# Infini-attention and MLP in one kernel: causal mask as half-array products, MLP output halves in tiles of their own, spare PSUM banks at the end, small work from VectorE to ScalarE, and a new order

## The chip, the cores and the metric

One core of a Trainium2 chip. The metric is the device time of one execution in microseconds (us), as the median of three runs. Lower is better.

## The reference

Inputs: q, k, v of shape (4, 8, 576, 64), a memory matrix `M_prev` and a norm `z_prev` for each head, a gate `beta`, and two matrices of an MLP, 512 x 2048 and 2048 x 512. Both stages work on all 4 x 576 = 2304 tokens.

```python
scores = scale * np.matmul(q, k.transpose(0, 1, 3, 2))
scores = np.where(causal, -1000000000.0, scores)
scores = scores - scores.max(-1, keepdims=True)
a = np.exp(scores); a /= a.sum(-1, keepdims=True) + 1e-09
local = np.matmul(a, v)
q_p = phi(q)                       # phi(x) = where(x > 0, x, exp(x) - 1) + 1
mem_out = einsum(q_p, M_prev) / (einsum(q_p, z_prev)[..., None] + 1e-06)
x = g * mem_out + (1 - g) * local  # g = sigmoid(beta), one per head; then heads side by side: (2304, 512)
h = x @ w_in
gelu = where(h >= 1, h, where(h <= -1, 0, (h + 1) ** 2 / 4))
out = gelu @ w_out
```

## The kernel before

**Numbers.** Every f32 operand of a product is split into two f16 tiles, a high and a low half ("hi" and "lo"), and a product is three f16 passes (`PASSES`). Splitting costs two passes over the data: `mul` writes hi (ScalarE, line 109, or VectorE, line 112) and `sub_scaled` writes lo (VectorE, line 116). Powers of two that keep f16 in range come from sums of squares (line 204, 328, 602).

**Work.** Weights come in 8 groups `W0` to `W7` (`weight_group`: three integer passes on VectorE at lines 201 to 203, then hi and lo). Heads come in 8 pairs of units (`P0` to `P7`, `prep`: hi and lo of q, k, v, M, and phi with its norm, lines 349 to 385) and 16 units of two heads. A unit has a half A (query tiles 0 and 1) and a half B (tiles 2, 3 and 4). For one query tile, `front` makes the scores on TensorE (line 413, or 439 and 441 for the short last tile; the two heads' products use 64 rows of the array each and run side by side), adds the causal mask with a product of `ident` and `mask` (line 458; all 128 rows), takes the row maximum on VectorE (line 462, 444), scales it (`negmax`, line 424, VectorE), and takes the exponential and its sum on ScalarE (line 428). `back` multiplies by the inverse sum and splits into hi and lo, and a DMA transposes them. `pv1` and `pv2` multiply with v (line 533; two 64-column halves side by side).

The MLP runs in 9 chunks `c0` to `c8` of 256 tokens, each over 8 groups of 256 hidden columns: 24 products into `h` (`mlp_h`, line 646, one PSUM bank, and there is one such bank), the activation in five passes (line 651 Relu and 652 Square on ScalarE, line 653 the clamp with max and min on VectorE, then hi on ScalarE and lo on VectorE; "16th Relu" below counts them in order of time), and 12 products into `o` (`mlp_o`, line 663, one tile of two banks). A chunk ends with two reads of `o` (line 690 or 692) and two output DMAs.

**Order.** The string `PROGRAM` lists the jobs, which only gives a first order. `in_order` then prices every instruction, plays the program forward and back under a list of blends, and fixes the order of each engine's own queue by the best round. Every engine runs its queue strictly in that order.

**Lines that the change touches.** Line 350 (`prep`) is the minimum of exp and 1 on VectorE; `negmax` is line 424; the mask products are lines 437 and 458; `halves` chooses the engine of hi by `OPT["hi"]`, which sends column groups 6 and 7 (the two heads of tile 3, 128 x 512) to VectorE; `mlp_h` and `chunk` hold the tiles `h` and `o`.

```python
OPT = dict(whi="act", phi="act", ghi="act", hi={6: "dve", 7: "dve"})
```

Of the kernel before, what the change touches and what calls it, by code (L numbers as in the profile page):

```python
# [49 lines left out]
def infini_moe_kernel(ctx: ExitStack, tc, qt, kt, qz, vm, beta, w, out):  # L50
# [92 lines left out]
    def setup_consts():  # L143
# [7 lines left out]
        nc.gpsimd.memset(mask, 0.0)  # L151
        nc.gpsimd.affine_select(out=mask, in_=mask, pattern=[[-1, P]], base=0,
                                channel_multiplier=1, compare_op=ALU.is_ge, fill=MASK)

        nc.gpsimd.tensor_copy(mask4[0:D], mask[0:D, 0:D])
        nc.gpsimd.tensor_copy(mask4[D:P], mask[D:P, D:P])
# [477 lines left out]
    def mlp_h(c, r, a, tb):  # L634
# [16 lines left out]
        nc.scalar.activation(tm, h, AF.Relu, bias=tb[:, 1, j:j + 1], scale=tb[:, 2, j:j + 1])  # L651
# [254 lines left out]
def in_order(tc, notes):  # L906
# [61 lines left out]
    for blend in BLENDS:  # L968
        times, taken = forward(urgency)
        end = max(t[1] for t in times)  # L970
        if end < best:
            best, order = end, taken
# [55 lines left out]
```

## Time and profile before

| | us |
|---|---|
| median of 3 runs (lowest to highest) | 617.37 (616.97 to 619.64) |
| the profiled execution's own time | 617.87 |
| its span, first to last instruction | 616.2 |
| busy: TensorE, VectorE, ScalarE | 521.7, 475.5, 451.8 |
| mean granted TensorE clock | 0.952 of full |

PE is TensorE's products, PEld its weight loads, DVE VectorE, ACT ScalarE, POOL GpSimd. A busy time is the time in which at least one instruction of the engine runs, so it is less than count times mean where instructions overlap. The profiled execution lies 0.50 us above the median, and its own time 1.67 us above its span.

### The profile page before, as it was taken

How to read it: one execution, taken by the hardware profiler on the slowest of the kernel's cores; microseconds unless marked ns; L12 is line 12 of the kernel's file. 1: busy time of each engine (PE TensorE's matmuls, PEld its weight loads, DVE VectorE, ACT ScalarE, POOL GpSimd, SP SyncE). 2: the span in 40 equal slices, each digit the busy share in tenths (PEclk: the TensorE clock that was granted, in tenths of full speed). 3: DMA queues.
4: the chain of work that ended last, by engine and by line, in shares of the span. 5: the costliest groups of instructions: out<-in, count | busy, mean ns of one | idle time of the engine just before them, and what ended most of it. 6: DMA issues, size and time to landing. Idle time of an engine off the chain costs nothing. (4 is left out here: it accounts for less than half of the span.)

```text
span 616.2 us, 11580 instructions
## 1 busy us (share of the span) xinstructions
PE 521.7 (85%) x4481; PEld 333.6 (54%) x4481; DVE 475.5 (77%) x1106; ACT 451.8 (73%) x916; POOL 2.5 (0%) x12
## 2 busy tenths in 40 slices
PE   0324565768699999999999999999999999999996
PEld 0112334444456566656665665666666666666663
DVE  5999999999999998497989849978677763223221
ACT  5768877769989987599797879769886765444433
POOL 1000000000000000000000000000000000000000
PEclk9997655799899999999999999999999999999999
DMA  7885984795542945348473526904362531000000
GB/s 307 294 273 135 231 207 126 201 216 212 145 103 62 183 95 97 91 124 199 134 160 63 112 59 154 220 3 83 69 106 50 126 67 32 35 1 2 35 0 35
DMA packets 130792, 74.68 MB, mean 121 GB/s; under 512 B 122289, under 2 KB 122289, under 8 KB 128689
## 3 DMA queue, kind: packets, MB, share of 16 engines
q1 hardware_dynamic: 130736, 73.94, 48.3%
q8 instruction: 35, 0.57, 0.4%
q14 instruction: 21, 0.16, 0.1%
HBM read 38.80 MB, written 4.72 MB: 71 GB/s over the span
## 5 line engine op out<-in xcount | busy, mean ns | idle before, releaser
L646 PE MATMUL h<-xh,w 128*128 128x256 f16 x1728 | 207.5, 276 | 12.8 <-DVE tm L653 12.1
L663 PE MATMUL o<-w,g 128*128 128x512 f16 x864 | 207.8, 379 | 6.7 <-DVE g L116 3.8
L646 PEld LDWEIGHTS <-w 128*128 128x128 f16 x1728 | 170.1, 99 | 51.3 <-issue 20.1
L663 PEld LDWEIGHTS <-g 128*128 128x128 f16 x864 | 80.7, 98 | 88.0 <-DVE g L116 5.3
L653 DVE SCALAR_TENSOR_TENSOR tm<-h,tb,tm 128x512 f32<-128x512 f32 x72 | 53.8, 747 | 68.7 <-ACT tm L652 64.2
L651 ACT ACTIVATE tm<-h,tb 128x512 f32<-128x512 f32 x72 | 55.8, 775 | 68.3 <-PE h L646 68.1
L428 ACT ACTIVATE e<-s,st,sc 128x256 f32<-128x256 f32 (+4 forms) x144 | 91.4, 638 | 13.4 <-DVE st L424 9.1
L116 DVE SCALAR_TENSOR_TENSOR an<-e,st,an 128x512 f16<-128x512 f32 (+4 forms) x160 | 80.8, 538 | 6.9 <-ACT an L109 6.9
L109 ACT ACTIVATE g<-tm,tb 128x512 f16<-128x512 f32 x72 | 51.8, 721 | 26.6 <-DVE tm L653 24.6
L116 DVE SCALAR_TENSOR_TENSOR g<-tm,tb,g 128x512 f16<-128x512 f32 x72 | 53.5, 746 | 18.9 <-ACT g L109 18.7
L109 ACT ACTIVATE an<-e,st 128x128 f16<-128x128 f32 (+3 forms) x112 | 56.0, 544 | 11.5 <-DVE st L478 3.8
L413 PE MATMUL s<-ks,qs 64*128 64x256 f16 (+3 forms) x384 | 43.4, 335 | 23.9 <-ACT e L428 8.8
L462 DVE TENSOR_REDUCE st<-s 128x2 f32<-128x256 f32 (+1 forms) x64 | 52.0, 816 | 5.5 <-PE s L458 5.3
L533 PEld LDWEIGHTS <-vs 128*64 128x64 f16 x1024 | 40.6, 118 | 17.0 <-issue 16.6
L652 ACT ACTIVATE tm<-tm 128x512 f32<-128x512 f32 x72 | 45.3, 629 | 1.0
L413 PEld LDWEIGHTS <-qs 64*128 64x128 f16 x384 | 16.1, 101 | 48.2 <-issue 27.3
L428 ACT ACTIVATION_READ_ACCUMULATOR e<-s,st,sc 128x1 f32 x144 | 28.9, 201 | 0.0
L533 PE MATMUL v<-eb,vs 128*64 128x256 f16 (+1 forms) x384 | 24.2, 276 | 2.1 <-DMA eb<-an 2.1
L533 PE MATMUL v<-pt,m 128*64 128x256 f16 (+1 forms) x192 | 19.2, 271 | 7.0 <-DMA pt<-pn 4.0
L307 PE MATMUL s<-sc,ones 128*128 128x4 f32 (+1 forms) x32 | 6.0, 263 | 21.9 <-ACT m L328 13.7
L109 ACT ACTIVATE w<-w,wsc 128x1024 f16<-128x1024 f32 x15 | 17.2, 1144 | 7.9 <-DVE nr L362 5.6
L204 ACT ACTIVATE stg<-w 128x1024 bf16<-128x1024 f32 x15 | 15.8, 1051 | 6.6 <-DVE w L203 6.4
(154 smaller groups left out, 575.7 us busy)
## 6 DMA issues: line engine op xcount, KB each, us to landing
stg<-w SPq DMA_DIRECT2D x16, 1024.0 KB, 5.5
rn<-qz SPq DMA_DIRECT2D x7, 768.0 KB, 5.3
rv<-vm SPq DMA_DIRECT2D x7, 768.0 KB, 5.0
rk<-kt SPq DMA_DIRECT2D x7, 576.0 KB, 4.1
rq<-qt SPq DMA_DIRECT2D x7, 576.0 KB, 5.0
out<-tm SPq DMA_DIRECT2D x14, 256.0 KB, 2.1
out<-part SPq DMA_DIRECT2D x4, 256.0 KB, 2.0
w<-vm SPq DMA_DIRECT2D x1, 768.0 KB, 13.8
```

What stands on the lines that cost most here:

```text
L109: return nc.scalar.activation(o, i, AF.Copy, scale=s)
L116: nc.vector.scalar_tensor_tensor(o, i, s, hi, op0=ALU.mult, op1=ALU.subtract)
L204: nc.scalar.activation(stage.bitcast(BF16)[:, 0:w.shape[3]], wt, AF.Square, accum_out=ss[:, m:m + 1])
L413: nc.tensor.matmul(s[:, h, a:a + n], u.pair.q[hs, tq, u.x, i * P:(i + 1) * P], u.pair.k[hs, tk, u.x, 0:n], start=first and j == 0, stop=False)
L428: nc.scalar.activation(e, s, AF.Exp, bias=st[:, 0, z:z + 1], scale=u.pair.cs, accum_out=st[:, 1, z:z + 1])
L462: nc.vector.tensor_reduce(st[:, 0, 2 * t:2 * t + 2], s[:, :, a:a + P * (t + 1)], axis=AX.X, op=ALU.max, negate=True)
L533: nc.tensor.matmul(pv[h * D:(h + 1) * D, a:c1], lhs, rhs, start=n < 2, stop=n >= len(terms) - 2)
L646: nc.tensor.matmul(h[:, u], w1[:, r, cc, wj, u * P:(u + 1) * P], x16[:, xj, cc, :], start=n == 0, stop=n == 3 * NCC - 1)
L651: nc.scalar.activation(tm, h, AF.Relu, bias=tb[:, 1, j:j + 1], scale=tb[:, 2, j:j + 1])
L652: nc.scalar.activation(tm, tm, AF.Square)
L653: nc.vector.scalar_tensor_tensor(tm, h, tb[:, 0, j:j + 1], tm, op0=ALU.max, op1=ALU.min)
L663: nc.tensor.matmul(acc[:, t], g16[:, gj, u, t * P:(t + 1) * P], w2[:, r * FPG + u, wj, :], start=(r == a and u == 0 and gj == 0 and wj == ...
```

## The change

1. The mask: `mask` (128 x 128) and `ident` give way to `pick` and `tri`. For each query tile and each of two 64-column halves z, one product for each head adds the mask, with 64 rows of the array and 64 columns: 256 products of 64 columns for 128 of 128.
2. `o` becomes two tiles `o0` and `o1` of one bank each, one for each half of the tokens.
3. In the last two chunks of `PROGRAM`, two of three groups take their `h` from a tile of the ring `s`, which the scores use before. In the very last group the activation is done in two halves.
4. VectorE to ScalarE: `negmax` in all 16 units (64 instructions); the minimum in `prep` (8 instructions; in its place ScalarE does Relu(-x) and then exp of its negative, so two passes where it did one); hi of column groups 6 and 7 (32 instructions).
5. `PROGRAM`, the number of rounds and three rounds with noise change, and so the order of all queues.

```diff
-OPT = dict(whi="act", phi="act", ghi="act", hi={6: "dve", 7: "dve"})
-PROGRAM = ("l0 l1 P0 W0 A0 A1 P1 A2 A3 p0 W1 B0 W2 B1 W3 c0/4 B2 B3 p1 W4 l2 c1/4 W5 W6 W7 c0 c1 P2 A4 A5 l3 P3 "
...
+OPT = dict(whi="act", phi="act", ghi="act", hi={6: "dve", 7: "dve"}, neg=16, relu=8, hia=16)
+SEEDS = ((54890, 300), (721312, 300), (836258, 1000))
+PROGRAM = ("l0 l1 P0 A0 A1 P1 W0 W1 B0 A2 A3 p0 B3 W2 B1 W3 c0/4 B2 p1 W4 c1/4 W5 W6 W7 c0 l2 P2 A5 c1 l3 P3 A4 "
...
-    mask = const.tile([P, P], BF16, name="mask")
-    mask4 = const.tile([P, D], BF16, name="mask4")
+    pick = [const.tile([P, P], BF16, name=f"pick{i}") for i in range(2)]
+    tri = [const.tile([P, D], BF16, name=f"tri{i}") for i in range(2)]
...
-        nc.scalar.activation(fe, u.qr, AF.Exp)
-        nc.vector.tensor_scalar(fe, fe, 1.0, None, op0=ALU.min)
+        if p < OPT["relu"]:
+            nc.scalar.activation(fe, u.qr, AF.Relu, scale=-1.0)
+            nc.scalar.activation(fe, fe, AF.Exp, scale=-1.0)
...
-        nc.vector.tensor_scalar(st[:, 0, a:a + m], st[:, 0, a:a + m], u.pair.cs, None, op0=ALU.mult)
+        mul("act" if u.n < OPT["neg"] else "dve", st[:, 0, a:a + m], st[:, 0, a:a + m], u.pair.cs)
...
-            for h in range(2):
-                nc.tensor.matmul(s[:, h, a + P * t:a + P * (t + 1)], ident, mask, start=False,
-                                 stop=t == tiles[-1][0])
+            for z in range(2):
+                for h in range(2):
+                    hs, c = slice(h * D, (h + 1) * D), a + P * t + D * z
+                    nc.tensor.matmul(s[:, h, c:c + D], pick[z][hs], tri[z][hs], start=False,
+                                     stop=z == 1 and t == tiles[-1][0])
...
-        mul(OPT["hi"].get(z, "act"), hi, e, r)
+        mul(OPT["hi"].get(z, "act") if u.n >= OPT["hia"] else "act", hi, e, r)
...
-        h = ps.tile([P, FPG, CT], F32, name=f"h{c}_{r}", tag="h")
+        if c in tail and r % 3:
+            if c not in more:
+                more[c] = ps.tile([P, 2, FPG, CT], F32, name=f"hm{c}", tag="s")
+            h = more[c][:, r % 3 - 1]
+        else:
+            h = ps.tile([P, FPG, CT], F32, name=f"h{c}_{r}", tag="h")
...
+        cuts = ((0, 1), (1, 2)) if c == tail[-1] and r == NG - 1 else ((0, FPG),)
+        for z0, z1 in cuts:
+            hz, tz, hi, lo = (x[:, z0:z1] for x in (h, tm, g16[:, 0], g16[:, 1]))
...
-            acc = ps.tile([P, 2, 512], F32, name=f"o{c}_{a}", tag="o")
+            acc = [ps.tile([P, DM], F32, name=f"o{t}{c}_{a}", tag=f"o{t}") for t in range(NTT)]
```

`tail` holds the last two chunks that `PROGRAM` names (8 and 7), and `mlp_o` writes `acc[t]`. The lines of the changed kernel differ: 445 is 428 of before, 111 is 109, 118 is 116, 681 and 682 are 651 and 652, 672 and 693 are 646 and 663, 720 is 690, 363 and 364 are the Relu and the exp of phi, 477 is the mask product.

The first place is ScalarE's queue in the middle of the program, in half B of a unit: `e` are exponentials, `an` the hi halves, `st` the row maxima, `h` the MLP's bank. Before:

```order
L428 ACTIVATE e_278,st_365<-s_157,st_365,sc_126 128x384 x2
L428 ACTIVATE e_221,st_365<-s_131,st_365,sc_126 128x512
L109 ACTIVATE an_283<-e_278,st_365 128x3x128 x2
L428 ACTIVATE e_221,st_365<-s_131,st_365,sc_126 128x512
L651 ACTIVATE tm_832<-h_192,tb_1243 128x512
L428 ACTIVATE e_278,st_365<-s_157,st_365,sc_126 128x576
L652 ACTIVATE tm_832<-tm_832 128x512
```

And in the change, in half B of a unit further on:

```order
L681 ACTIVATE tm_978<-h_396,tb_1304 128x512
L111 ACTIVATE g_1010<-tm_1095,tb_1304 128x512
L682 ACTIVATE tm_978<-tm_978 128x512
L111 ACTIVATE an_299<-e_294,st_550 128x576
L111 ACTIVATE an_238<-e_233,st_550 128x4x128 x2
L111 ACTIVATE stg_383<-v_251,sc_158 128x128
L111 ACTIVATE m_0_157<-rv_87,sc_333 128x256
L341 ACTIVATE qs_328,sc_1727<-rq_84 128x1152
L341 ACTIVATE ks_329,sc_1727<-rk_85 128x1152
L681 ACTIVATE tm_1009<-h_396,tb_1304 128x512
```

The two hi passes `an` of 128x4x128 (tile 3) now stand in ScalarE's queue between two Relus that free `h`; before they were VectorE's.

The second place is TensorE's queue where a tile's mask is added (`s` are score tiles, `g` and `o` MLP operands, `diag` the short tile's queries). Before:

```order
L413 MATMUL s_157<-ks_122,qs_121 128x512
L663 LDWEIGHTS g_833
L663 MATMUL o_800<-w_74,g_833 128x512
L458 LDWEIGHTS ident
L458 MATMUL s_157<-mask,ident 128x128
L437 LDWEIGHTS ident
L437 MATMUL s_131<-mask_66,ident 128x64
```

And in the change:

```order
L477 MATMUL s_189<-tri_67,pick_65 128x64
L477 LDWEIGHTS pick_66
L477 MATMUL s_189<-tri_68,pick_66 128x64
L430 LDWEIGHTS qs_328
L430 MATMUL s_163<-ks_329,qs_328 128x512
L477 LDWEIGHTS pick_66
L477 MATMUL s_189<-tri_68,pick_66 128x64
```

Before, the mask went in between products that use the whole array; now it goes in between score products that use it in halves, as it does itself.

The third place is the end of ScalarE's queue. Before:

```order
L651 ACTIVATE tm_918<-h_192,tb_1243 128x512
L652 ACTIVATE tm_918<-tm_918 128x512
L109 ACTIVATE g_876<-tm_918,tb_1243 128x512
L690 ACTIVATE tm_801<-o_800,tu_1244 128x512
L690 ACTIVATE tm_832<-o_800,tu_1244 128x512
```

And in the change:

```order
L681 ACTIVATE tm_1095<-s_189,tb_1304 128x256
L682 ACTIVATE tm_1095<-tm_1095 128x256
L681 ACTIVATE tm_1095<-s_189,tb_1304 128x256
L111 ACTIVATE g_1053<-tm_1095,tb_1304 128x256
L682 ACTIVATE tm_1095<-tm_1095 128x256
L111 ACTIVATE g_1053<-tm_1095,tb_1304 128x256
L720 ACTIVATE tm_1009<-o_0_977,tu_1305 128x512
L720 ACTIVATE tm_978<-o_0_976,tu_1305 128x512
```

The last activation is in two halves (its `h` is a score tile, `s_189`), and the two reads of the output are now of two tiles.

## Rows read from the trace of the kernel before

**Rows 1.** The page, part 2: the span in 40 equal slices, busy share in tenths, and the granted TensorE clock in tenths.

```profile
DVE  5999999999999998497989849978677763223221
...
PEclk9997655799899999999999999999999999999999
```

**Rows 2.** Busy time of each engine in five stretches, cut at the 1st, 7th, 16th and 37th Relu of the MLP and at the end of the last product into `h` (instruction counts in brackets; columns as the heading row has them).

```profile
core 0: us, PE busy (x) PEld busy (x) DVE busy (x) ACT busy (x) POOL busy (x), PEclk, DMA share, GB/s
0.00:108.70 108.70, 44.99 (x364) 26.56 (x366) 99.73 (x229) 77.85 (x167) 2.49 (x12) 0.78 0.75 224
108.70:165.40 56.70, 41.78 (x371) 27.17 (x371) 56.70 (x116) 47.00 (x88) 0.00 (x0) 0.91 0.74 204
165.40:228.80 63.40, 58.92 (x514) 38.02 (x516) 62.99 (x167) 56.70 (x123) 0.00 (x0) 1.00 0.50 109
228.80:382.50 153.70, 150.84 (x1352) 95.33 (x1353) 126.44 (x309) 125.71 (x259) 0.00 (x0) 1.00 0.53 118
382.50:605.40 222.90, 219.70 (x1863) 144.50 (x1862) 128.13 (x287) 141.13 (x277) 0.00 (x0) 1.00 0.28 59
```

**Rows 3.** What VectorE waited for in the first 230 us: us in total, times, longest.

```profile
DVE pn L350 <- ACT pn L349: 5.2, 1, 5.2
...
DVE sc L308 <- PE s L307: 0.8, 1, 0.8
```

**Rows 4.** ScalarE's groups up to 229.5 us: the MLP's Relu, and how many of them (busy us, mean ns, idle before).

```profile
L651 ACT ACTIVATE tm<-h,tb 128x512 f32<-128x512 f32 x16 | 12.4, 772 | 4.8 <-PE h L646 4.7
```

**Rows 5.** One row of ScalarE's timeline: the 16th of those Relus (start us, us).

```profile
228.81 0.78 ACT L651 ACTIVATE tm<-h,tb 128x512 f32<-128x512 f32 x1 [1.30 <-PE h L646]
```

**Rows 6.** VectorE's groups up to 229.5 us, shapes apart: the work that moves (busy us, mean ns).

```profile
L112 DVE TENSOR_SCALAR an<-e,st 128x512 f16<-128x512 f32 x12 | 5.4, 483 | 0.0
...
L350 DVE TENSOR_SCALAR pn<-pn 128x1152 f32<-128x1152 f32 x5 | 3.8, 753 | 5.2 <-ACT pn L349 5.2
...
L424 DVE TENSOR_SCALAR st<-st,sc 128x2 f32<-128x2 f32 x12 | 2.5, 219 | 0.0
...
L424 DVE TENSOR_SCALAR st<-st,sc 128x4 f32<-128x4 f32 x8 | 1.7, 218 | 0.0
...
L424 DVE TENSOR_SCALAR st<-st,sc 128x1 f32<-128x1 f32 x6 | 1.2, 207 | 0.0
```

**Rows 7.** VectorE's timeline, 226.3 to 227.9 us: where instructions follow each other, the next starts before the last ends (start us, us).

```profile
226.32 1.21 DVE L354 TENSOR_TENSOR pn<-rn 128x1024 f32<-128x1024 f32 x1
227.44 0.48 DVE L112 TENSOR_SCALAR an<-e,st 128x512 f16<-128x512 f32 x1
227.84 0.15 DVE L476 SCALAR_TENSOR_TENSOR st<-st,cg 128x1 f32<-128x1 f32 x1
```

**Rows 8.** ScalarE's groups, whole run, shapes apart: the nearest rows to the work that arrives there.

```profile
L109 ACT ACTIVATE g<-tm,tb 128x512 f16<-128x512 f32 x72 | 51.8, 721 | 26.6 <-DVE tm L653 24.6 <-PE o L663 1.3 <-DVE tb L629 0.5
...
L349 ACT ACTIVATE pn<-rn 128x1152 f32<-128x1152 f32 x7 | 8.1, 1155 | 3.4 <-DMA rn<-qz 3.4
...
L208 ACT ACTIVATE wssb<-wss 128x2 bf16<-128x2 f32 x8 | 1.6, 200 | 0.1
```

**Rows 9.** ScalarE's timeline near 13.5 us: a small instruction and the start of the next.

```profile
13.53 0.20 ACT L365 ACTIVATE nq<-nr 128x18 f32<-128x18 f32 x1
13.64 0.19 ACT L365 ACTIVATION_READ_ACCUMULATOR nq<-nr 128x1 f32 x1
```

**Rows 10.** TensorE's timeline, 480.4 to 481 us (start us, us, products).

```profile
480.39 0.28 PE L458 MATMUL s<-mask,ident 128*128 128x128 bf16 x2
480.50 0.38 PE L663 MATMUL o<-w,g 128*128 128x512 f16 x1
480.81 0.25 PE L533 MATMUL v<-pt,m 128*64 128x64 f16 x4
480.99 0.39 PE L663 MATMUL o<-w,g 128*128 128x512 f16 x1
```

**Rows 11.** TensorE's timeline, 496.1 to 500.7 us (the output products of one half B).

```profile
496.08 0.63 PE L533 MATMUL v<-ec,vs 128*64 128x64 f16 x28
496.54 0.39 PE L533 MATMUL v<-pt,m 128*64 128x256 f16 x4
...
497.90 2.79 PE L646 MATMUL h<-xh,w 128*128 128x256 f16 x24
```

**Rows 12.** TensorE's groups from 228.8 to 605.4 us: the mask products.

```profile
L458 PE MATMUL s<-mask,ident 128*128 128x128 bf16 x72 | 9.2, 222 | 0.0
```

**Rows 13.** What TensorE waited for: products into `h` behind the clamp that frees their bank, in the whole run.

```profile
PE h L646 <- DVE tm L653: 12.1, 15, 4.6
```

**Rows 14.** The same from 520 to 606 us.

```profile
PE h L646 <- DVE tm L653: 1.4, 2, 0.8
```

**Rows 15.** The end of the run in order of time (start us, us; in brackets the idle time before and what ended it).

```profile
605.42 0.78 ACT L651 ACTIVATE tm<-h,tb 128x512 f32<-128x512 f32 x1 [2.23 <-PE h L646]
...
608.46 0.61 PE L663 MATMUL o<-w,g 128*128 128x512 f16 x2 [0.48 <-ACT g L109]
...
609.25 2.33 PE L663 MATMUL o<-w,g 128*128 128x512 f16 x10 [0.18 <-DVE g L116]
611.62 1.27 ACT L690 ACTIVATE tm<-o,tu 128x512 f32<-128x512 f32 x2 [3.21 <-PE o L663]
```

More of the change, by code (lines that the diff above doesn't have):

```diff
@@ L150, in setup_consts @@
                                 channel_multiplier=1, compare_op=ALU.is_equal, fill=0.0)
[L151 to L156, printed above, removed]
+        for i in range(2):
+            nc.gpsimd.memset(pick[i], float(i))
+            nc.gpsimd.memset(tri[i], 0.0)
+        for hs in (slice(0, D), slice(D, P)):
+            nc.gpsimd.affine_select(out=pick[0][hs], in_=pick[0][hs], pattern=[[-1, P]], base=0,
+                                    channel_multiplier=1, compare_op=ALU.not_equal, fill=1.0)
+            nc.gpsimd.affine_select(out=pick[1][hs], in_=pick[1][hs], pattern=[[-1, P]], base=D - 1 - P * (D - 1),
+                                    channel_multiplier=P, compare_op=ALU.is_ge, fill=0.0)
+            nc.gpsimd.affine_select(out=pick[1][hs, D:P - 1], in_=pick[1][hs, D:P - 1], pattern=[[-1, D - 1]], base=0,
+                                    channel_multiplier=1, compare_op=ALU.not_equal, fill=1.0)
+            for t in tri:
+                nc.gpsimd.affine_select(out=t[hs], in_=t[hs], pattern=[[-1, D]], base=0,
+                                        channel_multiplier=1, compare_op=ALU.is_ge, fill=MASK)
+            nc.gpsimd.affine_select(out=tri[1][hs], in_=tri[1][hs], pattern=[[0, D]], base=D - 2,
+                                    channel_multiplier=-1, compare_op=ALU.is_ge, fill=MASK)
         for t in diag:
@@ L594, in infini_moe_kernel @@
     mlp = {}
+    tail, more = [int(t[1:].split("/")[0]) for t in PROGRAM.split() if t[0] == "c"][-2:], {}
     def chunk_prep(c):
@@ L650, in mlp_h @@
         kind(f"c{c}", "ev")
[L651 to L655 removed]
+        cuts = ((0, 1), (1, 2)) if c == tail[-1] and r == NG - 1 else ((0, FPG),)
+        for z0, z1 in cuts:
+            hz, tz, hi, lo = (x[:, z0:z1] for x in (h, tm, g16[:, 0], g16[:, 1]))
+            nc.scalar.activation(tz, hz, AF.Relu, bias=tb[:, 1, j:j + 1], scale=tb[:, 2, j:j + 1])
+            nc.scalar.activation(tz, tz, AF.Square)
+            nc.vector.scalar_tensor_tensor(tz, hz, tb[:, 0, j:j + 1], tz, op0=ALU.max, op1=ALU.min)
+            mul(OPT["ghi"], hi, tz, tb[:, 3, j:j + 1])
+            sub_scaled(lo, tz, tb[:, 3, j:j + 1], hi)
         return g16
@@ L967, in in_order, with passes @@
     best, order = math.inf, None
[L968 to L972, printed above, removed]
-        back, _ = backward([-t[1] for t in times])
-        middle = sum(t[0] for t in times) / n
-        urgency = [blend * (t[0] - middle) - b[1] for b, t in zip(back, times)]
+    def passes(urgency, blends):
+        nonlocal best, order, chosen
+        for blend in blends:
+            times, taken = forward(urgency)
+            end = max(t[1] for t in times)
+            if end < best:
+                best, order, chosen = end, taken, urgency
+            back, _ = backward([-t[1] for t in times])
+            middle = float(np.mean([t[0] for t in times]))
+            urgency = [blend * (t[0] - middle) - b[1] for b, t in zip(back, times)]
+    chosen = urgency
+    passes(urgency, BLENDS)
+    for seed, width in SEEDS:
+        noise = np.random.default_rng(seed).normal(size=n) * width
+        passes([u + float(x) for u, x in zip(chosen, noise)], BLENDS[:6])
     last = {}
```

25 lines of the change are left out of this document (12 added, 13 removed).

## The prediction

> **What bounds the kernel now.** The strip of 40 slices comes first [rows 1]: VectorE stands at 9 or more through the first 15 slices but one and thins out only afterwards, and TensorE's clock is at 5 to 7 tenths only there. The table of busy times then gives the border [rows 2]. Up to the 16th Relu of the MLP VectorE is busy 99.73 of 108.70 us, 56.70 of 56.70 and 62.99 of 63.40: 9.4 us of idle time in 228.8, and 5.2 of them are the wait for the first exp, with under a microsecond for the next [rows 3]. TensorE meanwhile is idle for 83. So the first 228.8 us last as long as VectorE's queue. The 16th Relu is the mark because 16 start by 229.5 [rows 4], the last at 228.81 [rows 5]. Afterwards it is TensorE: 150.84 of 153.70 and 219.70 of 222.90, at full clock, while VectorE and ScalarE have 18% and more to spare [rows 2]. So what leaves VectorE counts in the first stretch, what leaves TensorE in the second, and what comes to ScalarE must fit beside both.
>
> **VectorE's queue up to the 16th Relu.** The table of its groups has the work that goes: 12 hi passes, 5 minima and 26 scalings of the row maximum (12 + 8 + 6) [rows 6]. On a queue without gaps an instruction costs the distance to the next start, not its duration: the hi passes of 0.48 us are 0.40 apart from what follows, and 1.21 us at 226.32 end in a next start 1.12 later [rows 7]. I take 0.08 off every mean: 12 x 0.40 + 5 x 0.67 + 26 x 0.13 = 4.8 + 3.4 + 3.4 = 11.6 us. Summed row by row at such prices up to its 16th clamp, the changed VectorE queue is 16.8 us shorter; the other 5 are one pair's phi stage and some lo passes, put off to where VectorE has room. So 16.8 us is the most that this stretch can give.
>
> **What ScalarE takes of that.** Its prices: a hi pass of 128x512 takes 0.72 us, a pass of 128x1152 1.155, a small one 0.20 [rows 8]; a small instruction's distance to the next is 0.11 [rows 9], so again 0.09 off: 0.63, 1.06 and 0.11. By the 16th Relu the changed queue holds 10 hi passes more (6.3), 26 scalings (2.9) and 8 passes of phi for 5 (3.2), less 1.8 of other work that stands later: 10.6 more. 13.4 more stand before the first Relu, so between the first and the 16th it holds 2.8 less, 100.9 for 47.00 + 56.70 = 103.7 [rows 2]. The fullest that ScalarE has been is 56.70 of 63.40, 0.894 [rows 2]. If VectorE's whole saving were taken, ScalarE would have to be busy 100.9 of 105.8, or 0.95; at 0.894 it needs 112.9 us, 7.2 fewer than 120.1. Before the first Relu (77.85 of 108.70, so 91 after) it has room, and VectorE's 2.5 count in full. **I take 7.2 + 2.5 = 9.7 us less**, with 16.8 as the one end and, if ScalarE's waits grow with its load, 3 as the other.
>
> What the hi pass shows is a bad exchange by itself: 0.72 us on ScalarE [rows 8] for 0.48 on VectorE [rows 6]. The Trainium skill, "ScalarE: Activation LUTs", section "Rules for kernel authors", says to give multiplications, minima and maxima to VectorE and not to ScalarE. By that rule the moves should not be made; the trace agrees on the prices, and rival A is what it would do here.
>
> **The start.** VectorE begins when the first exp is done, after 5.2 us of waiting [rows 3]. Now a Relu of 1.155 us [rows 8] stands ahead of that exp: 1.1 us more, covered by nothing. POOL takes some 16 small steps for the mask instead of 4; the first mask is needed after k and q are split, which is later. On SP two weight loads stand one place earlier. I cost both at nothing: POOL has no other work, and ScalarE's prep of the first pair covers the loads.
>
> **TensorE after the 16th Relu.** A product into `o` is 0.217 us from the next (the last ten: (2.33 - 0.38) / 9 [rows 15]), but at 480.50, where half-array products follow, 0.31 [rows 10]: a change between whole and half array costs 0.094 us. Along the whole queue the changes fall from 221 to 182, after the 16th Relu from 131 to 117: 14 x 0.094 = 1.3 us less. The mask of a tile takes 0.11 us now, two products [rows 10]. For the new kind the nearest row is 28 half-array products of 64 columns in 0.46 us [rows 11], 0.033 for a pair, so 0.066 for the four. 36 tiles are left (72 products [rows 12]): 36 x 0.044 = 1.6 us less. The bounds are 1.6 less and, if no two run side by side, four times 0.033, 0.7 more. Against it the changed queue leaves one half B's output products (496.08 to 497.90, 1.8 us [rows 11]) for after the 16th Relu, and three products into `o` fewer (0.6): 1.2 more. **Net 1.7 us less.** Before the 16th Relu these savings fall into TensorE's idle time and count nothing.
>
> On the mask one rule says otherwise. The Trainium skill, "TensorEngine Tiling (Array Packing)", section "Instruction Overhead", gives each product about 60 cycles of overhead and advises against splitting a dimension that is small already. By its figure, as an estimate, four products would take about 0.1 us at 2.4 GHz, and the mask would gain nothing. The 0.033 for a pair of 64 columns, instead of twice 0.025, is what speaks against that here.
>
> **The two tiles of `o`.** No product into `o` in the list of waits stands behind a read of it, so there is nothing to take away until the end. Nothing.
>
> **Spare banks.** Products into `h` wait 12.1 us for the clamp that frees the one bank [rows 13], but 1.4 in the last two chunks [rows 14], where the banks are added: **1.4 less**.
>
> **The end.** After the last product into `h` TensorE works off the group before, stands 0.48 + 0.18 us, and ScalarE then reads two outputs in 1.27 [rows 15]. With two tiles the first read moves beside the last products: 0.6 less. The halves of the last activation are almost in series, since the second Relu stands behind the first half's clamp in the order, but 13 products (2.8 us) cover them, and TensorE's gap goes: 0.6 less. **1.2 less**, between nothing and 2.
>
> **The sum.** -9.7 + 1.1 - 1.7 - 1.4 - 1.2 = -12.9 us on the profiled execution's 617.87, so 605.0; that execution lies 0.5 above the median, so 604.5 for a median.
>
> **Rivals.**
> A. ScalarE becomes the bound in the middle. From the 16th to the 37th Relu its changed queue holds 17.3 us more: 143.0 for 125.71 in 153.70 us [rows 2]. At the share of 0.894 that is 160.0 us, 6.3 longer: 610.8. For it: TensorE has no idle time there that could hide a late Relu. Against: 0.894 was reached while VectorE set the pace and need not be a limit.
> B. ScalarE does run at 0.95, and VectorE's whole 16.8 us come through: 597.4. For it: up to now ScalarE waits there for others.
> C. Slower: the one bank of `h` turns too slowly. Until the last two chunks the Relu and Square that free it stand in ScalarE's queue, now behind hi passes and scalings. The 22 hi passes and 38 scalings after the 16th Relu are 22 x 0.63 + 38 x 0.11 = 18.0 us; if each delays the bank while TensorE has nothing else, that is 622.5. It decides once TensorE's wait for the clamp grows from 12.1 us [rows 13] to more than 25. Against: before, that wait was small in the middle, since attention products fill in.
> D. The gains are used up on the way: VectorE, TensorE and ScalarE are all near full between the first and the 16th Relu, and waits among them, or a longer time at half clock, take back all but 3 us: 614.3 to 620.5.
> E. The mask's halves don't run side by side: 2.3 us more than summed, 606.8, still within the forecast's own range of 599 to 609.
>
> **Chances.** Forecast with E 0.53, A 0.18, B 0.13, D 0.09, C 0.07. A measurement of this kernel can tell about 0.5% (3.1 us) from no change: faster takes the forecast, A and B, 0.84; same is D, 0.09; slower is C, 0.07. The range goes from 596, below B, to 613, above A; some 0.16 lies above and little below.
>
> **What would show it.** VectorE's busy time down by the durations that go (64 x 0.22 + 8 x 0.75 + 32 x 0.48, about 35) to 441, ScalarE's up by 40 or so; no wait of VectorE in the first 215 us but the first; the 16th Relu at 217 to 223 us instead of 228.8; mask products two at a time, 0.03 us from pair to pair; 182 changes of the array's mode; after the 16th Relu TensorE still over 97% busy. Wrong would be: VectorE with gaps before the 16th Relu (A early, or D), TensorE's idle time behind the clamp over 25 us (C), or a gain that comes from after the 16th Relu.

## Result: 599.7 us, 3.0% less, and the profile after

| | before | after |
|---|---|---|
| median, us (lowest to highest) | 617.48 (616.97 to 619.64) | 599.71 (598.43 to 599.83) |
| ratio, 95% interval | | 0.970 (0.967 to 0.973) |
| profiled execution; its span | 617.87; 616.2 | 598.43; 596.7 |
| busy: TensorE, VectorE, ScalarE | 521.7, 475.5, 451.8 | 510.8, 450.6, 489.0 |
| start of the 1st, 16th, 37th Relu | 108.7, 228.8, 382.5 | 109.0, 216.3, 367.8 |
| start of the last group's (first) Relu to the end | 10.7 | 9.7 |

Medians and ratios, here and below, leave out two stray executions that took three to five times as long as the others, one of the kernel before (2874 us) and one of a_dve_first (1799 us).

The forecast was 604.5 us, in a range of 596 to 613. The direction and the places held; the gain was under-estimated by 5 us.

Busy time of each engine, cut at the same marks as [rows 2] (1st, 7th, 16th and 37th Relu, the end of the last product into `h`), and the end as a sixth stretch (columns as there):

```profile
0.00:109.00 109.00, 43.60 (x413) 28.35 (x413) 100.31 (x220) 91.85 (x203) 5.18 (x24) 0.78 0.86 241
109.00:155.30 46.30, 37.10 (x343) 25.82 (x342) 45.11 (x94) 40.69 (x76) 0.00 (x0) 0.93 0.73 213
155.30:216.30 61.00, 58.24 (x502) 37.92 (x501) 58.78 (x148) 59.52 (x135) 0.00 (x0) 1.00 0.47 111
216.30:367.80 151.50, 148.06 (x1481) 97.96 (x1481) 125.75 (x291) 143.20 (x310) 0.00 (x0) 1.00 0.57 122
367.80:587.00 219.20, 217.94 (x1856) 144.87 (x1851) 118.80 (x253) 149.69 (x297) 0.00 (x0) 1.00 0.28 58
587.00:596.70 9.70, 5.83 (x28) 2.36 (x25) 1.85 (x4) 4.09 (x8) 0.00 (x0) 1.00 0.15 54
```

Up to the 16th Relu VectorE is busy 100.31 + 45.11 + 58.78 = 204.2 us of 216.3, where [rows 2] gave 219.4 of 228.8. ScalarE is busy 192.1 instead of 181.6, and between the 7th and the 16th Relu 59.52 of 61.00 us. TensorE still fills what follows: 148.06 of 151.50 and 217.94 of 219.20. So 12.5 of the 19.5 us of span are gone before the 16th Relu, 5.9 from there to the last product into `h` (376.6 before, 370.7 now), 1.1 at the end.

The page's strips of 40 slices, against [rows 1]:

```profile
DVE  4999999999999989969968679598667653423222
ACT  5887998988999999989999899789888676444534
...
PEclk9998656898999999999999999999999999999999
```

VectorE stands at 9 from the 2nd to the 14th slice, as before; ScalarE is at 8 or 9 from the 5th to the 25th, which reaches past the 16th Relu (slice 15). The granted clock falls to 5 tenths in the same early slices as before.

What VectorE waited for up to the 16th Relu, against [rows 3] (us in total, times, longest):

```profile
DVE rn L369 <- ACT pn L364: 6.3, 1, 6.3
DVE an L118 <- ACT an L111: 1.8, 2, 1.6
DVE tm L683 <- ACT tm L682: 1.0, 1, 1.0
```

The first wait grew from 5.2 us by the Relu now ahead of the exp; two small waits for ScalarE are new. The 16th Relu, against [rows 5], in ScalarE's timeline:

```profile
216.30 0.81 ACT L681 ACTIVATE tm<-h,tb 128x512 f32<-128x512 f32 x1
```

The scalings of the row maximum on ScalarE, in its timeline (start us, us), against the instruction they were priced by in [rows 9]:

```profile
204.68 0.31 ACT L111 ACTIVATE st<-st,sc 128x1 f32<-128x1 f32 x1
204.86 0.64 ACT L682 ACTIVATE tm<-tm 128x512 f32<-128x512 f32 x1
```

The next start comes 0.18 us later, not 0.11. The groups of the work that arrived on ScalarE, whole run, shapes apart (busy us, mean ns of one | idle time before):

```profile
L111 ACT ACTIVATE an<-e,st 128x512 f16<-128x512 f32 x32 | 22.4, 722 | 1.7 <-ACT e L445 1.0 <-DMA ea<-an 0.7
...
L111 ACT ACTIVATE st<-st,sc 128x2 f32<-128x2 f32 x32 | 9.4, 295 | 6.0 <-DVE st L481 5.9
...
L111 ACT ACTIVATE st<-st,sc 128x1 f32<-128x1 f32 x16 | 4.8, 298 | 1.0 <-DVE st L461 0.9
```

The hi pass costs 722 ns, as in [rows 8]; a scaling costs 295 to 298 ns instead of 200. TensorE's wait for the clamp that frees the bank of `h`, whole run, against [rows 13]:

```profile
PE h L672 <- DVE tm L683: 6.4, 13, 1.5
```

It fell from 12.1 to 6.4 us, and in the last 88 us of the run no such wait is left, where [rows 14] had 1.4.

### The profile page after: what moved, and what is told of

The parts are those of the page before. It is cut to its first block, busy times and chain, and to the rows that moved or that the text cites. A ratio compares the mean times of both kernels' runs of the same rounds, so it can differ in the third digit from the quotient of the medians.

```text
span 596.7 us, 11893 instructions
## 1 busy us (share of the span) xinstructions
PE 510.8 (86%) x4609; PEld 337.3 (57%) x4609; DVE 450.6 (76%) x1004; ACT 489.0 (82%) x1023; POOL 5.2 (1%) x24
## 5 line engine op out<-in xcount | busy, mean ns | idle before, releaser
L672 PE MATMUL h<-xh,w 128*128 128x256 f16 x1488 | 184.6, 278 | 12.7 <-DVE tm L683 6.4
L445 ACT ACTIVATE e<-s,st,sc 128x128 f32<-128x128 f32 (+4 forms) x144 | 91.9, 641 | 1.9 <-DVE an L118 0.9
L111 ACT ACTIVATE an<-e,st 128x128 f16<-128x128 f32 (+4 forms) x144 | 78.2, 587 | 4.0 <-ACT e L445 2.3
L118 DVE SCALAR_TENSOR_TENSOR g<-tm,tb,g 128x512 f16<-128x512 f32 (+1 forms) x73 | 53.9, 739 | 26.9 <-ACT g L111 24.5
L111 ACT ACTIVATE g<-tm,tb 128x512 f16<-128x512 f32 (+1 forms) x73 | 52.3, 718 | 15.2 <-DVE tm L683 15.1
L430 PE MATMUL s<-ks,qs 64*128 64x256 f16 (+3 forms) x384 | 41.6, 334 | 18.9 <-ACT e L445 14.4
L481 DVE TENSOR_REDUCE st<-s 128x2 f32<-128x256 f32 (+3 forms) x64 | 51.5, 813 | 5.8 <-PE s L477 5.8
L682 ACT ACTIVATE tm<-tm 128x512 f32<-128x512 f32 (+1 forms) x73 | 45.7, 627 | 0.8
L672 PE MATMUL s<-xh,w 128*128 128x256 f16 x240 | 32.2, 273 | 0.0
L681 ACT ACTIVATE tm<-s,tb 128x512 f32<-128x512 f32 (+1 forms) x11 | 8.1, 738 | 27.0 <-PE s L672 26.4
L111 ACT ACTIVATE st<-st,sc 128x2 f32<-128x2 f32 (+2 forms) x64 | 18.7, 296 | 8.9 <-DVE st L481 7.8
```

The costliest lines, as they stand in the source:

```text
L111: return nc.scalar.activation(o, i, AF.Copy, scale=s)
L118: nc.vector.scalar_tensor_tensor(o, i, s, hi, op0=ALU.mult, op1=ALU.subtract)
L430: nc.tensor.matmul(s[:, h, a:a + n], u.pair.q[hs, tq, u.x, i * P:(i + 1) * P], u.pair.k[hs, tk, u.x, 0:n], start=first and j == 0, stop=False)
L445: nc.scalar.activation(e, s, AF.Exp, bias=st[:, 0, z:z + 1], scale=u.pair.cs, accum_out=st[:, 1, z:z + 1])
L481: nc.vector.tensor_reduce(st[:, 0, 2 * t:2 * t + 2], s[:, :, a:a + P * (t + 1)], axis=AX.X, op=ALU.max, negate=True)
L672: nc.tensor.matmul(h[:, u], w1[:, r, cc, wj, u * P:(u + 1) * P], x16[:, xj, cc, :], start=n == 0, stop=n == 3 * NCC - 1)
```

## Experiments

Theory V: VectorE's queue sets the time up to the 16th Relu, so what left it made the gain. Rival O: the new list and rounds made the order, and the order made the gain. Two kinds of run: with the **order kept** (each engine's queue is that of the kernel named, an instruction only changes engine or form) and **planned anew** (the kernel's own planner orders the edited program). "Busy" counts up to the 16th Relu of the profiled execution, which is called the mark below.

| run | order | median us | ratio to before (95%) | 16th Relu | VectorE busy | ScalarE busy |
|---|---|---|---|---|---|---|
| before | | 617.5 to 618.2 | 1 | 228.8 | 219.4 | 181.6 |
| after | | 599.71 | 0.970 (0.967 to 0.973) | 216.3 | 204.2 | 192.1 |
| a_moves_off | kept, of after | 614.84 | 0.995 (0.992 to 0.997) | 226.5 | 214.4 | 179.4 |
| b_moves_on | kept, of before | 632.92 | 1.025 (1.022 to 1.027) | 231.2 | 210.4 | 198.8 |
| order_only | new | 612.75 | 0.991 (0.989 to 0.992) | 228.5 | 219.6 | 184.5 |
| parts_only | new, old list | 614.93 | 0.994 (0.992 to 0.996) | 230.9 | 216.0 | 207.2 |
| moves_off_plan | new | 608.26 | 0.985 (0.983 to 0.986) | 228.7 | 219.0 | 181.4 |
| mask_old | new | 608.31 | 0.984 (0.982 to 0.986) | 222.2 | 205.8 | 194.9 |
| no_seeds | new | 598.85 | 0.969 (0.968 to 0.971) | 219.7 | 206.7 | 194.6 |
| no_banks | new | 602.98 | 0.976 (0.975 to 0.978) | 225.7 | 211.9 | 201.4 |
| a_mask_old | kept, of after | 602.30 | 0.975 (0.973 to 0.978) | 221.6 | 204.6 | 192.3 |
| a_dve_first | kept, of after | 612.75 | 0.991 (0.990 to 0.993) | 230.6 | 217.7 | 192.7 |
| a_act_first | kept, of after | 606.84 | 0.982 (0.981 to 0.984) | 225.0 | 205.4 | 204.4 |
| moves_early | new | 603.88 | 0.977 (0.975 to 0.979) | 219.1 | 208.1 | 193.9 |

### Parts against order

**a_moves_off.** The three moves undone, the change's order kept.

```diff
-OPT = dict(..., hi={6: "dve", 7: "dve"}, neg=16, relu=8, hia=16)
+OPT = dict(..., hi={6: "dve", 7: "dve"}, neg=0, relu=0, hia=0)
```

> The changed kernel with its order of all queues held fixed, and the three kinds of moved work (scaling of the row maximum, the minimum of phi, the hi passes of tile 3) put back on VectorE at the same places of the order. Theory V (up to the 16th Relu the run lasts as long as VectorE's queue, so the moves made the gain): VectorE's queue up to there is 11.6 us longer again, the 16th Relu at 226 to 230 us instead of 216.3, the time 609 to 613 us. Rival O (the new order made the gain; ScalarE is so full that the moves are worth nothing): within 3 us of 599.7.

**b_moves_on.** The three moves made in the kernel before, its order kept.

```diff
-OPT = dict(whi="act", phi="act", ghi="act", hi={6: "dve", 7: "dve"})
+OPT = dict(whi="act", phi="act", ghi="act", hi={})
...
-        nc.scalar.activation(fe, u.qr, AF.Exp)
-        nc.vector.tensor_scalar(fe, fe, 1.0, None, op0=ALU.min)
+        nc.scalar.activation(fe, u.qr, AF.Relu, scale=-1.0)
+        nc.scalar.activation(fe, fe, AF.Exp, scale=-1.0)
...
-        nc.vector.tensor_scalar(st[:, 0, a:a + m], st[:, 0, a:a + m], u.pair.cs, None, op0=ALU.mult)
+        mul("act", st[:, 0, a:a + m], st[:, 0, a:a + m], u.pair.cs)
```

> The kernel before with its order of all queues held fixed, and the same three kinds of work given to ScalarE at the same places of the order; mask, output tile and banks as before. Theory V: 8 to 11 us of the 11.6 come off before the 16th Relu, 606 to 610 us. Rival O: 615 us or more, since ScalarE gets 35 us of work at places that were not laid out for it.

**order_only.** The kernel before with the change's list, rounds and noise.

```diff
-BLENDS = (-0.1,) * 24
-PROGRAM = ("l0 l1 P0 W0 A0 A1 P1 A2 A3 p0 W1 B0 W2 B1 W3 c0/4 B2 B3 p1 W4 l2 c1/4 W5 W6 W7 c0 c1 P2 A4 A5 l3 P3 "
+BLENDS = (-0.1,) * 20
+SEEDS = ((54890, 300), (721312, 300), (836258, 1000))
+PROGRAM = ("l0 l1 P0 A0 A1 P1 W0 W1 B0 A2 A3 p0 B3 W2 B1 W3 c0/4 B2 p1 W4 c1/4 W5 W6 W7 c0 l2 P2 A5 c1 l3 P3 A4 "
...
```

> The kernel before in all its parts, its order planned anew with the changed list of jobs, rounds and noise. Theory V: VectorE still has all its work before the 16th Relu, so 611 to 618 us. Rival O: 605 us or less.

**parts_only.** The change with the old list and rounds: the same diff the other way round.

> All parts of the change (mask, output tiles, banks, cut, moves), its order planned with the old list of jobs and the old 24 rounds without noise. Theory V: 599 to 606 us. Rival O: 612 us or more.

Neither theory stands alone. Undoing the moves in the change's order costs 15.1 us, more than V's range of 609 to 613 us allows, and making them in the old order costs another 15, where V had expected a gain. Order alone gains 5, as V had it; all parts with the old list gain 3, in O's range and not in V's; both together gain 18. The stretches of b_moves_on up to its 37th Relu (columns as above) show what went wrong there:

```profile
0.00:108.10 108.10, 43.43 (x364) 25.11 (x366) 93.99 (x206) 87.12 (x190) 2.48 (x12) 0.87 0.75 225
108.10:167.00 58.90, 42.92 (x371) 27.83 (x367) 56.13 (x109) 50.30 (x95) 0.00 (x0) 0.86 0.72 200
167.00:231.20 64.20, 59.01 (x514) 37.87 (x516) 60.26 (x154) 61.34 (x136) 0.00 (x0) 1.00 0.48 105
231.20:393.70 162.50, 152.02 (x1357) 95.84 (x1358) 122.16 (x278) 138.50 (x291) 0.00 (x0) 1.00 0.50 112
```

VectorE is busy 9.0 us less than before up to the 16th Relu, and the mark still comes 2.4 later. The list of its waits up to there:

```profile
DVE rn L352 <- ACT pn L350: 9.5, 3, 6.4
DVE an L116 <- ACT an L109: 5.4, 8, 1.2
DVE st L476 <- ACT e L428: 2.4, 4, 1.0
```

The first wait was 5.2 us and the others under a microsecond in [rows 3]. From the 16th to the 37th Relu the old order then takes 162.50 us against 153.70 [rows 2], with TensorE idle for 10.5 of them. TensorE's wait for the clamp that frees `h` is 19.3 us in its whole run, 12.1 in [rows 13]. In an order made for the old parts, the work put on ScalarE delays what VectorE and TensorE wait for. That is the way of rivals A and C, but not their size: ScalarE is busy 138.50 of the 162.50 us, 0.85, below A's 0.894, and 19.3 us is short of the 25 that C set.

In parts_only the old list puts more of both engines' work ahead of the mark than the change's list does, 11.8 us on VectorE and 15.1 on ScalarE, and between the first and the 16th Relu both are busy for 0.95 or more of 129.0 us:

```profile
0.00:101.90 101.90, 38.98 (x336) 25.29 (x337) 93.02 (x200) 82.65 (x180) 4.81 (x24) 1.00 0.82 236
101.90:170.10 68.20, 47.69 (x495) 33.27 (x494) 67.61 (x152) 64.33 (x135) 0.00 (x0) 0.85 0.76 202
170.10:230.90 60.80, 58.17 (x557) 38.29 (x552) 55.38 (x134) 60.20 (x135) 0.00 (x0) 1.00 0.53 101
```

So the order also decides how much work has to be done before the mark. In a_moves_off, where VectorE has its old work back in the new order, its three stretches up to the 16th Relu, and the two from there to the last product into `h`, are:

```profile
0.00:114.00 114.00, 44.86 (x443) 29.35 (x445) 106.76 (x244) 83.14 (x179) 5.18 (x24) 0.85 0.81 230
114.00:162.10 48.10, 37.03 (x316) 25.55 (x311) 46.06 (x98) 38.31 (x71) 0.00 (x0) 0.89 0.67 205
162.10:226.50 64.40, 60.09 (x499) 38.45 (x498) 61.62 (x158) 57.98 (x125) 0.00 (x0) 0.97 0.45 104
226.50:382.60 156.10, 148.66 (x1483) 97.88 (x1483) 135.47 (x327) 130.66 (x273) 0.00 (x0) 1.00 0.55 119
382.60:606.00 223.40, 218.44 (x1856) 144.79 (x1853) 125.70 (x281) 139.56 (x269) 0.00 (x0) 1.00 0.27 57
```

10.2 us more of VectorE, and the mark 10.2 us later. But the profiled execution, the longest of 12 (612.7 to 617.4 us), takes 18.9 us more than the change's, and 8.8 of them are lost between the mark and the last product into `h` (379.5 us against 370.7), where V had nothing. TensorE is idle for 12.4 us there, instead of 4.7, and ScalarE's exponentials wait in this stretch for scalings that are VectorE's again (us in total, times, longest):

```profile
ACT e L445 <- DVE st L114: 22.7, 21, 2.8
```

So the 15.1 us hold, beside what VectorE's queue costs, what an order made for the other engines costs; the two are not measured apart.

### The moves, with the order free to adapt

**moves_off_plan.** The edit of a_moves_off, planned anew.

> The change, but with the row-maximum scalings, the minima of phi and the hi passes of tile 3 left on VectorE, and the order planned anew for that (the earlier run with the moves undone kept the change's order). Theory J (the moves and the order each give little alone, because the order has to put the moved work where ScalarE has room; with the order free to adapt, undoing the moves costs only what VectorE's queue grows by): between 605 and 610 us, 16th Relu at 222 to 228 us, VectorE busy about 216 to 220 us up to it as in the kernel before. Rival P (the change's list and noise rounds are a lucky order, and the moves are worth nothing once the order is free): within 3 us of the change, 597 to 603, 16th Relu at 215 to 219. Rival V alone (the moves are worth the whole 15 us even with a free order): 612 to 617.

```profile
0.00:112.30 112.30, 41.37 (x413) 27.20 (x414) 104.64 (x239) 81.24 (x175) 4.93 (x24) 0.92 0.77 229
112.30:168.00 55.70, 40.13 (x344) 27.28 (x344) 54.86 (x113) 44.62 (x87) 0.00 (x0) 0.88 0.62 187
168.00:228.70 60.70, 59.69 (x525) 38.32 (x525) 59.51 (x155) 55.54 (x119) 0.00 (x0) 1.00 0.48 111
```

Theory J held: 608.26 us, VectorE busy 104.64 + 54.86 + 59.51 = 219.0 us and the 16th Relu at 228.7 (0.7 later than J's range), both as before, though list, mask, banks and end are new. Against after, undoing the moves costs 8.6 us with a free order and 15.1 with a fixed one. Between the two profiled executions the mark is 12.4 us later, and 2.6 come back behind it. Read as a chain: list and rounds 5.1 us (order_only), the mask, the banks and the end 4.5 more (moves_off_plan), the moves 8.6. Each step of the chain is a new plan, so each may hold some 6 us of the plan's own (mask_old below).

**no_seeds.** `SEEDS = ()` in the change.

> The change with its three noise rounds of the order left out, the rest planned as it is: how much of the time is the choice of one order among similar ones. Theory J expects a few us: 600 to 605, with ScalarE's share between the first and the 16th Relu still above 0.93. If the order chosen by the noise is what makes the moves pay, 607 to 615, near the run with the parts and the old list.

598.85 us, just under J's 600 to 605: the noise rounds are worth nothing that shows, and another order reaches the same time. J's other sign fails: ScalarE's share between the first and the 16th Relu is 0.90, not above 0.93. The mark comes 3.4 us later than in the change, and the profiled execution is only 1.7 longer. Orders differ in how much TensorE has done by the mark (141.6 us here, 138.9 in the change), so from one order to another a later mark need not count in full.

**moves_early.** The moves in units 0 to 7 only.

```diff
-OPT = dict(..., neg=16, relu=8, hia=16)
+OPT = dict(..., neg=8, relu=8, hia=8)
```

> The change with the scalings of the row maximum and the hi passes of tile 3 moved to ScalarE only in units 0 to 7; units 8 to 15 keep them on VectorE; planned anew. By the prediction's own rule (what leaves VectorE counts up to the 16th Relu, which is reached in unit 6 or 7; afterwards TensorE is the bound): within 3 us of the change, 597 to 602.5, VectorE busy about 461 us and ScalarE about 467. If the late moves carry part of the gain: 604 to 607. If ScalarE holds TensorE up after the 16th Relu, and this relieves it: below 597.

603.88 us, 4.2 above the change and between the two expectations of 597 to 602.5 and 604 to 607; VectorE's busy time came out as said (461.6), ScalarE's did not (474.1 for 467). Of the 5.5 us between the two profiled executions 2.8 are lost before the 16th Relu, where both kernels have moved the same 10 hi passes and 25 scalings, so they are the new plan's, and 2.7 after. Whether the late moves are worth those 2.7 us stays open.

### The two engines' load, one at a time

**a_dve_first** and **a_act_first.** In the change's order, 32 extra instructions of 128 x 256, in units 0 to 3, on VectorE or on ScalarE:

```diff
+        if u.n in (0, 1, 2, 3):
+            nc.vector.scalar_tensor_tensor(junk, junk, ones32[:, 0:1], junk, op0=ALU.mult, op1=ALU.subtract)
```

```diff
+        if u.n in (0, 1, 2, 3):
+            nc.scalar.activation(junk, junk, AF.Copy, scale=ones32[:, 0:1])
```

> The change with its own order and 32 more instructions of 128 x 256 on VectorE, one before each lo pass of the exponentials in units 0 to 3, at about 0.40 us each on the queue, so 12.7 us more of VectorE before the 16th Relu; their output is not used. Theory V (VectorE's queue is the clock up to the 16th Relu): 16th Relu at 225 to 229 us and 608 to 612 us in all. If VectorE's 12 us of idle time there take it up: 600 to 604 us.

> The same 32 extra instructions on ScalarE in the same places, about 12.7 us more of ScalarE before the 16th Relu; their output is not used. ScalarE had 24 us of idle time up to the 16th Relu, nearly all before the 7th. If ScalarE is a bound beside VectorE (its share of 0.976 between the 7th and the 16th Relu): 16th Relu at 222 to 229 us and 605 to 612 us in all. If it only fills the gaps that VectorE leaves: 600 to 603 us.

Their groups (mean ns of one) and the first three stretches, first for VectorE:

```profile
L507 DVE SCALAR_TENSOR_TENSOR junk<-junk,ones 128x256 f32<-128x256 f32 x32 | 15.4, 480 | 0.3
```

```profile
0.00:120.90 120.90, 45.79 (x445) 29.84 (x447) 112.40 (x249) 92.16 (x203) 5.44 (x25) 0.82 0.77 217
120.90:169.60 48.70, 37.44 (x317) 25.70 (x310) 46.55 (x97) 40.99 (x76) 0.00 (x0) 0.89 0.68 202
169.60:230.60 61.00, 58.23 (x502) 37.93 (x501) 58.79 (x148) 59.55 (x136) 0.00 (x0) 1.00 0.47 110
```

Then for ScalarE, with what VectorE waited for up to the 16th Relu:

```profile
L507 ACT ACTIVATE junk<-junk,ones 128x256 f32<-128x256 f32 x32 | 16.2, 505 | 0.0
```

```profile
0.00:117.30 117.30, 42.88 (x459) 28.44 (x461) 101.89 (x220) 102.93 (x232) 5.43 (x25) 0.83 0.80 224
117.30:164.10 46.80, 34.59 (x300) 23.92 (x296) 44.83 (x94) 41.93 (x80) 0.00 (x0) 0.96 0.75 209
164.10:225.00 60.90, 58.10 (x502) 37.83 (x500) 58.69 (x147) 59.52 (x136) 0.00 (x0) 1.00 0.48 112
```

```profile
DVE rn L371 <- ACT pn L366: 6.4, 1, 6.4
DVE an L118 <- ACT an L111: 4.7, 8, 1.6
DVE w L371 <- ACT pn L366: 2.8, 1, 2.8
```

Next starts come 0.396 us (VectorE) and 0.399 us (ScalarE) after these instructions, so 12.7 and 12.8 us were added, 30 of the 32 before the first Relu. On VectorE they moved the first Relu by 11.9 us, one for one (30 x 0.396 = 11.9), the 16th by 14.3 and the time by 13.0, both just above V's ranges, and nothing after the mark changed. That is V, as a measurement; why the stretch from the first to the 7th Relu grew by 2.4 us for 0.8 us of added work stays open. On ScalarE they moved the mark by 8.7 and the time by 7.1, although ScalarE had been busy only 91.85 of the first 109.00 us. VectorE's waits name the way: `an` from ScalarE, 1.8 us before and 4.7 now, and 2.8 us for a phi pass that it had not waited for. In this order ScalarE is a second bound in the first stretch already, at a busy share of 0.84.

### The mask and the banks

**mask_old.** Whole-array mask products again, planned anew.

```diff
-            for z in range(2):
-                for h in range(2):
-                    hs, c = slice(h * D, (h + 1) * D), a + P * t + D * z
-                    nc.tensor.matmul(s[:, h, c:c + D], pick[z][hs], tri[z][hs], start=False, ...
+            for h in range(2):
+                nc.tensor.matmul(s[:, h, a + P * t:a + P * (t + 1)], ident, mask, start=False, ...
```

> The change, but the causal mask is added by whole-array products of the identity and the 128 x 128 mask again; planned anew. After the 16th Relu the trace of the change has score products 3.8 us shorter in all and mask products as long as before in all, and 13 fewer turns of the array. If these come from the mask's form, the time is 602 to 605 us (3 to 5 more than the change), the score products that follow mask products go back to about 92 ns each, and TensorE is busy about 4 us longer after the 16th Relu. If the turns fell because of the order, the time stays within 2 us of the change (598 to 602). The prediction's own term was 1.6 to 2.9 us.

**a_mask_old.** The same edit in the change's own order.

> The change with its own order kept on every engine; only the mask of a tile is two whole-array products of the identity and the 128 x 128 mask in the place of the first two of its four half-array products. Theory M (the mask's form is worth its TensorE time after the 16th Relu and nothing before it): 602 to 605 us, 16th Relu within 2 us of the change's 216.3, some 3 to 5 us more from there to the end. Rival N (the 8 us of the run that was planned anew were the order's): 599 to 601. If the mask also counts before the 16th Relu, where TensorE has idle time: 606 to 609 with the 16th Relu at 219 or later.

Planned anew the edit cost 8.6 us, more than any theory had; in the same order 2.6, which is in M's range. So some 6 us of mask_old are its plan's, and the size of any one run planned anew, moves_off_plan among them, is uncertain by as much. TensorE's busy time after the mark is 4.0 us longer in mask_old, as expected there. M's split did not come out: after the 16th Relu the profiled execution takes 381.9 us, 1.5 more than the change where M had 3 to 5, and it lost 5.3 us before the mark. The runs of this kernel spread from 600.5 to 605.3, and the profiled one took 605.2. Of the 5.3 us 3.8 lie between the first and the 7th Relu, where the granted TensorE clock was 0.86, against 0.93 in the change, and VectorE waited 2.8 us for a weight's DMA, against 0.2; how much of them is the mask's can't be said.

TensorE at one mask in the change, six score products, four mask products and one into `o` (start us, us):

```profile
333.03 0.66 PE L430 MATMUL s<-ks,qs 64*128 64x384 f16 x6
333.53 0.22 PE L477 MATMUL s<-tri,pick 64*128 64x64 bf16 x4
333.69 0.39 PE L693 MATMUL o<-w,g 128*128 128x512 f16 x1
```

And the same place in a_mask_old:

```profile
338.92 0.66 PE L434 MATMUL s<-ks,qs 64*128 64x384 f16 x6
339.51 0.28 PE L479 MATMUL s<-mask,ident 128*128 128x128 bf16 x2
339.63 0.38 PE L695 MATMUL o<-w,g 128*128 128x512 f16 x1
```

From scores to `o` 0.66 us against 0.71. The mask starts 0.50 us after the scores instead of 0.59: the change of mode ahead of it is gone. The four products then take 0.16 us up to the next, instead of 0.12, because the change now lies behind them: they start in pairs 28 ns apart in the trace, at 333.531 and 333.559, two by two. From start to start, after the 16th Relu, 276 score products take 27.1 us in a_mask_old and 23.7 in the change, the mask products 5.6 and 5.3, and the changes of mode are 130 and 117. So the mask's form is worth 3.7 us from start to start there; 2.2 of them show in TensorE's busy time (374.0 against 371.8), 1.5 in the time from the mark to the end.

**no_banks.** `if c in tail and r % 3:` never taken.

> The change without the spare banks for h in the last two chunks (the halves of the last activation stay); planned anew. By the prediction's term (the wait of TensorE for the clamp in the last two chunks was 1.4 us before) 601 to 603 us, with TensorE's wait for the clamp in the last 80 us back at 1 to 2 us. If the banks only give the planner room and TensorE has other work there: within 1 us of the change.

602.98 us, but the 16th Relu comes at 225.7, 9.4 us later than in the change and far ahead of the edit, and TensorE's waits for the clamp in the last 88 us are nil without the banks too. The 1.4 us of wait are gone for another reason, the order; what the banks are worth isn't told by this run.

## Why the prediction was right in direction and too small

**What bounds the kernel**: right. VectorE's queue up to the 16th Relu (a_dve_first, 11.9 us of delay for 11.9 us added before the first Relu), TensorE afterwards (over 97% busy). On the profiled execution the sum said -12.9 us and the span fell by 19.5: 3.9 of the 6.6 us that are missing lie before the mark, 2.8 between it and the last product into `h`.

**VectorE's queue, up to 16.8 us**: 15.2 measured in busy time. **ScalarE's load, 10.6 us more** by the 16th Relu: 10.5 measured, by two errors that cancel: the 25 scalings took 5.0 us and not 2.9, since each costs 0.19 and not 0.11, and some 3.7 us of other work fell away up to there, not 1.8.

**The step that failed** is the one that turned these into time: "at 0.894 it needs 112.9 us" between the first and the 16th Relu. It took 107.3, with ScalarE at 0.934, and at 0.976 from the 7th on. 0.894 was the share ScalarE had while VectorE set the pace, and no limit; the prediction said so itself under A and took the number all the same. The companion step, "before the first Relu it has room, and VectorE's 2.5 count in full", failed the other way: the first Relu was due at 108.7 - 2.5 + 1.1 = 107.3 and came at 109.0, and a_act_first shows that at a share of 0.84 there was little room. Together -12.5 instead of -8.6. Rival B (597.4) had this term nearer than the forecast. What neither had is the order: the sum counted what each queue holds and not where it stands, and at unplanned places the same moves make the kernel 15 us slower (b_moves_on). Rival C's wait grows in that kernel (19.3 us, short of its 25) and falls in this one (6.4).

**The start**: +1.1 predicted, the wait went from 5.2 to 6.3.

**TensorE after the 16th Relu**: -1.7 predicted, about -4.5 measured in busy time. The mask and the turns were put at 1.6 + 1.3 = 2.9; the runs show 3.7 in a fixed order and, from before to after, 33.0 to 29.0 us for scores and masks. Pairs run side by side as assumed (28 ns a pair, 33 taken), so E fell (its price, 0.7 us more for the mask, is 0.8 by the prediction's own figures). The rest is the term "1.2 more left for later": 54 more products with v (+1.7 us from start to start) but 5 fewer into `o` (-1.3) and the sums of squares 1.0 less.

**Spare banks**: -1.4 predicted; TensorE's idle time between the mark and the end of the last `h` fell by 6.06 - 4.70 = 1.4. The size is right, the cause isn't shown (no_banks).

**The end**: -1.2 predicted, -1.1 measured, both halves as worked out:

```profile
586.84 5.99 PE L693 MATMUL o<-w,g 128*128 128x512 f16 x27
587.04 0.56 ACT L681 ACTIVATE tm<-s,tb 128x256 f32<-128x256 f32 x1 [0.93 <-PE s L672]
...
588.61 0.56 ACT L681 ACTIVATE tm<-s,tb 128x256 f32<-128x256 f32 x1 [0.55 <-DVE tm L683]
...
592.22 1.33 ACT L720 ACTIVATE tm<-o,tu 128x512 f32<-128x512 f32 x2 [1.20 <-PE o L693]
```

The 27 products into `o` now run without a gap, where 0.48 + 0.18 us stood in [rows 15], because the second half's activation is done beside them. The first of the two reads starts at 592.22, 0.61 us before the last product ends at 592.83; before, it started 0.04 after.

**What would show it.** VectorE's busy time was to fall by 35 to 441 and fell by 24.9 to 450.6: there I subtracted durations, where neighbours overlap. At the distances used in the sum, 64 x 0.13 + 8 x 0.67 + 32 x 0.40 = 26.5, it comes out. The 16th Relu came at 216.3, just under the 217 to 223 given. VectorE was to wait only once in the first 215 us; it waits 1.8 and 1.0 us more for ScalarE. ScalarE's busy time rose by 37.2 us for the 40 given, and the changes of mode fell to the 182 given. A gain from after the 16th Relu was to be a sign of being wrong: 7.0 of the 19.5 us came there, nearly the share that the sum itself had put there (4.3 of 12.9).

**Rival A** fell: from the 16th to the 37th Relu 151.5 us instead of 153.7, with ScalarE at 143.20, 0.945.

The Trainium skill, "ScalarE: Activation LUTs", section "Rules for kernel authors", gives multiplications and minima to VectorE. Here keeping to it cost 8.6 us with a new plan (moves_off_plan), some of which may be the plan's, and 15.1 in the change's order (a_moves_off), and in the order of the kernel before it was worth 15 (b_moves_on). The trace agrees that a hi pass is dearer on ScalarE, 722 ns against 483 [rows 6].

## What to carry to other kernels

Where two engines share a queue's work, price a move by the engine that paces the stretch, but test the other by adding load to it: its busy share is neither a limit (0.894 became 0.976) nor a measure of room (at 0.84 two thirds of the added load came through). A move and the order made for it are one change: each alone gave 3 to 5 us or lost 15, both together gave 18, so compare both at fixed queues and planned anew, and expect several us of chance from any new plan. Subtract distances between starts, not durations, wherever instructions of an engine overlap.

## What the runs showed of the hardware

- A ScalarE instruction on 2 columns with a scale that is read from a tile takes 0.295 us, and the next starts 0.188 us after it; with an immediate scale it was 0.20 and 0.11 [rows 9]. The Trainium skill, "ScalarE: Activation LUTs", section "What ACT_TABLE_LOAD costs", puts the immediate form at 186 ns (and 0.833 for each element) and each operand of one value per partition at 93 ns more, with 93 ns of overlap. That makes, as an estimate, 0.281 us for the instruction and 0.188 to the next start; the trace agrees to 0.014 us, and by it the 26 scalings would have been priced at 4.9 us instead of 2.9.
- Half-array products of 64 columns start in pairs 28 ns apart in the mask shown, so its four products take 56 ns of TensorE's queue, and the change of mode comes behind them and not ahead of them. Where more half-array products follow it is saved: 117 changes after the 16th Relu, against 130 with the whole-array mask in the same order. The Trainium skill, "TensorEngine Tiling (Array Packing)", section "Instruction Overhead", with about 60 cycles for each product, would make them, as an estimate, 100 ns one after the other; the trace has a pair in the time of one such product.
- Two engines at 92 and 84% of a stretch can both bound it, in a fixed order: 30 x 0.396 = 11.9 us more on the one moved the first Relu by 11.9 us, 30 x 0.399 = 12.0 on the other by 8.3.
